# MLP weights fetched in 14 pieces spread over steps, in place of four transfers back to back

## Chip, cores, metric

The kernel runs on one core of a Trainium2 chip. The metric is the device time of one execution in microseconds (us); a run is an execution timed alone, and the profile is one execution taken by the hardware profiler. A run counts as slow when it is more than 1.5% above the fastest of the same kernel.

## The reference

A transformer block with modulation (cut; `mod` is six rows of `silu(c) @ w_mod`):

```
h = layernorm(x) * (1 + ca) + sa
x = x + ga * attention(h)      # 32 query heads, 8 kv heads, last 512 keys of the caches, head size 128; then @ wo
h = layernorm(x) * (1 + cb) + sb
x = x + gb * (relu(h @ w1) @ w2)   # w1 512 x 1792, w2 1792 x 512
```

There are 2048 rows of 512, all in bfloat16. A fast path and a general path are in the program; these inputs take the fast path, and only it is dealt with here.

## The kernel before

The rows go in 4 blocks of 512, each with 32 heads: 128 steps, one for each head and block. In a step PE computes scores, projects q for the head two steps on, does P·V of the previous head and adds up to four "background" matmuls. The background is mostly the output projection, in groups of eight heads (`HQ = 8`):

```python
for s in range(NU):                      # NU = 128 steps
    run_tasks(s, 100)                    # loads, layer norms, ... that are due at step s
    ...                                  # cut: enqueue an output projection that is ready
    s_mms(s, 0)
    if s + QA < NU:
        q_mms(s + QA)
    s_mms(s, 1)
    if s >= 1:
        pv_mms(s - 1)                    # P.V of head s-1, division on DVE, transpose by DMA
    pop_bg(4)                            # up to four output-projection matmuls
```

A head's output is divided on DVE, and the SP queue then transposes it by DMA. All that goes through SP is issued in program order:

```python
def pv_mms(u):
    ...                                  # cut: 16 matmuls into o_ps, reciprocal
    kb.op(DVE, ... o_sb[u % NOS] ...)    # NOS = 4
    dma(oT[u % NOT][:, :, :], o_sb[u % NOS]..., f"oT{u % NOT}",
        reads=[R_o[u % NOS]], writes=[R_oT[u % NOT]], transpose=True)
    if (u + 1) % HQ == 0:
        wo_ready.append((u + 2, b, h // HQ))   # group of eight: usable two steps later
```

The MLP weights land in the tile that held the modulation weights (`wmw`). They are loaded at steps 60 and 64, long before the MLP, in four transfers of 896 KB:

```python
def load_w1():
    for i in range(2):
        f0, f1 = i * FC // 2, (i + 1) * FC // 2            # FC = 14
        dma(w1_sb[:, :, f0 * P:f1 * P], w1v[:, :, f0 * P:f1 * P], f"w1{i}", writes=R_w1[f0:f1] + R_wm)

def load_w2():
    for i in range(2):
        f0, f1 = i * FC // 2, (i + 1) * FC // 2
        dma(w2_sb[:, f0:f1, :], w2v[:, f0:f1, :], f"w2{i}", writes=R_w2[f0:f1] + R_wm)

add(60, load_w1)
add(64, load_w2)
```

`writes=... + R_wm` is there so that a load waits for the last reader of the modulation weights. It has a second effect: each load is now the latest writer of `R_wm`, and the next load must wait until it has landed. That wait is on SP, ahead of everything that SP issues later.

## Time and profile before

| | before |
|---|---|
| time, median of 3 runs | 570.52 us (569.95 to 571.03) |
| span of the profiled run | 568.2 us |
| PE busy | 553.0 us, 97% |
| PE's one named wait between 14 and 560 us | 2.1 us, for the DMA oT<-o |
| weight loads | 4 x 896 KB, 5.2 us to landing |

A line of the timeline gives start, length, engine, source line, operation, output<-inputs and count; in square brackets stands how long the engine was idle before it and what ended that. PE is matmul, DVE the vector engine, SPq the queue of SyncE. "To landing" is the time from the start of a DMA's issue until its data is there; the length of an SPq row is the issue alone. Where a row covers several instructions its length runs from the first to the last.

### The profile page before, as it was taken

The page shows a single profiled execution, that of the slowest core. Times are in us where ns is not written, and L with a number is a line of the kernel's source. Part 1 is how long each engine was busy: PE and PEld are TensorE (multiplying, and loading weights), DVE is VectorE, ACT ScalarE, POOL GpSimd, SP SyncE. Part 2 cuts the span into 40 slices and gives each one's busy share as a digit, 9 for nine tenths or more (in the row PEclk, how much of TensorE's full clock was granted, in tenths as well). Part 3 has the DMA queues.
Part 4 walks back from the last instruction along what each step waited for, and adds up shares of the span by engine and source line. Part 5 has one row for each costly group of instructions (what it writes and reads, how often), then busy time and mean ns, then how long its engine had stood idle before and what let it go on. Part 6 is the DMA issues. An engine that isn't in the chain of part 4 may idle for free.

```text
span 568.2 us, 9662 instructions
## 1 busy us (share of the span) xinstructions
PE 553.0 (97%) x4094; PEld 318.7 (56%) x4169; DVE 242.9 (43%) x532; ACT 347.3 (61%) x445; POOL 38.7 (7%) x41
## 2 busy tenths in 40 slices
PE   6999999999999999989999999999999999999997
PEld 5565555666655555546666555555555654444443
DVE  4344465533334655323336553333354438322133
ACT  2876666666666666656666666666666654432500
POOL 1000000002300000023000000330000000000000
PEclk8999999999999999999999999999999999999999
DMA  8795768331231145742321432121114220210001
GB/s 227 202 192 119 179 131 171 81 74 38 39 76 38 38 81 124 167 108 42 75 39 37 75 75 39 38 38 38 38 37 67 47 39 1 38 38 22 22 28 47
DMA packets 111620, 42.67 MB, mean 75 GB/s; under 512 B 94032, under 2 KB 111184, under 8 KB 111568
## 3 DMA queue, kind: packets, MB, share of 16 engines
q1 hardware_dynamic: 110752, 41.70, 34.4%
q8 instruction: 34, 0.56, 0.4%
q10 hardware_dynamic: 816, 0.26, 0.2%
q14 instruction: 18, 0.15, 0.1%
HBM read 18.35 MB, written 2.10 MB: 36 GB/s over the span
## 4 chain that ended last, share of the span: by engine, by line
PE 96%; DMA 2%; DVE 1%; issue 1%; ACTq 0%
PE psS L1350 28%; PE psO L1350 26%; PE psQ L1350 23%; PE psW L1350 19%; DMA oT<-o 1%; DMA x<-in_A_x_dram 1%; DVE st L1360 0%; PE psS L1353 0%; DVE hT L1397 0%; DVE PT L1631 0%; DVE PT L1632 0%; DVE mv L1361 0%; DVE o L1475 0%; ACTq L1296 0%; DVE xn L1371 0%
## 5 line engine op out<-in xcount | busy, mean ns | idle before, releaser
L1464 ACT ACTIVATE PT<-psS 128x1024 bf16<-128x1024 f32 x256 | 262.8, 1028 | 131.7 <-PE psS L1350 131.7
L1350 PE MATMUL psS<-qT,kT 128*128 128x512 bf16 x509 | 151.2, 379 | 0.2
L1350 PEld LDWEIGHTS psO<-v,PT 128*128 128x128 bf16 x2048 | 126.6, 98 | 30.2
L1350 PE MATMUL psO<-v,PT 128*128 128x129 bf16 x2048 | 137.0, 220 | 0.0
L1350 PE MATMUL psQ<-hT,wq 128*128 128x512 bf16 x507 | 130.8, 381 | 1.1 <-DVE hT L1397 1.1
L1474 DVE RECIPROCAL rinv<-psO 128x4 f32<-128x4 f32 x128 | 23.3, 182 | 234.5 <-PE psO L1350 234.5
L1350 PE MATMUL psW<-wo,oT 128*128 128x512 bf16 x451 | 118.1, 379 | 5.3 <-DMA oT<-o 2.1
L1475 DVE TENSOR_TENSOR o<-psO,rinv 128x512 bf16<-128x512 f32 x128 | 88.5, 691 | 4.7 <-DVE rinv L1474 0.3
L1350 PEld LDWEIGHTS psQ<-hT,wq 128*128 128x128 bf16 x508 | 49.7, 98 | 61.1 <-issue 1.0
L1350 PEld LDWEIGHTS psS<-qT,kT 128*128 128x128 bf16 x512 | 49.7, 98 | 59.5 <-ACT PT L1464 0.7
L1456 ACT ACTIVATE qT<-psQ 128x512 bf16<-128x512 f32 x127 | 75.4, 593 | 1.2 <-PE psQ L1350 1.2
L1350 PEld LDWEIGHTS psW<-wo,oT 128*128 128x128 bf16 x512 | 44.9, 98 | 35.4 <-DMA oT<-o 2.6
L1620 ACT ACTIVATE wq<-psS 128x512 bf16<-128x512 f32 x56 | 33.4, 597 | 49.2 <-PE psS L1350 49.2
L1497 DVE TENSOR_TENSOR acc<-psW,acc 128x512 f32<-128x512 f32 x48 | 33.1, 690 | 9.0 <-PE psW L1350 9.0
L1350 PE MATMUL psO<-wmw,wq 128*128 128x512 bf16 x136 | 31.0, 379 | 0.3
L1366 POOL TENSOR_TENSOR rstd<-rstd,cst 128x4 f32<-128x4 f32 (+2 forms) x9 | 8.6, 961 | 273.5 <-DVE rstd L1365 273.4
L1500 POOL TENSOR_TENSOR acc<-acc,gaf 128x512 f32<-128x512 f32 x12 | 15.2, 1268 | 171.0 <-DVE acc L1497 171.0
L1350 PE MATMUL psS<-h2T,wmw 128*128 128x512 bf16 x110 | 25.2, 379 | 0.1
L1350 PE MATMUL psS<-hT,wmw 128*128 128x512 bf16 x110 | 24.4, 379 | 0.1
L1631 DVE TENSOR_TENSOR PT<-psO,gbf 128x512 f32<-128x512 f32 x10 | 6.9, 691 | 40.2 <-PE psO L1350 40.2
L1360 DVE BATCH_NORM_STATS2 st<-x 128x6 f32<-128x512 bf16 x32 | 21.7, 680 | 4.6 <-DMA x<-in_A_x_dram 4.6
L1350 PEld LDWEIGHTS psO<-wmw,wq 128*128 128x128 bf16 x140 | 13.7, 98 | 16.5
(60 smaller groups left out, 168.8 us busy)
## 6 DMA issues: line engine op xcount, KB each, us to landing
wo<-in_A_wo_dram SPq DMA_DIRECT2D x4, 1024.0 KB, 5.9
wq<-in_A_wq_dram SPq DMA_DIRECT2D x7, 512.0 KB, 5.8
wmw<-in_B_w_dram SPq DMA_DIRECT2D x4, 896.0 KB, 5.2
wmw<-in_w_mod_dram SPq DMA_DIRECT2D x6, 512.0 KB, 5.2
oT<-o SPq DMA_TRANSPOSE x128, 2.4
out_dram<-PT SPq DMA_DIRECT2D x16, 128.0 KB, 1.7
x<-in_A_x_dram SPq DMA_DIRECT2D x3, 512.0 KB, 4.2
v<-in_A_v_cache_dram SPq DMA_DIRECT2D x8, 128.0 KB, 4.6
```

The lines of the kernel that those rows point to most:

```text
L1350: kb.op(PE, lambda e: e.matmul(out_ap, lhsT, rhs, start=start, stop=stop), reads=reads, group_writes=[R_b[k] for k in bk], signal=signal)
L1360: kb.op(DVE, lambda e: e.bn_stats(st[:, t, :], x_sb[:, t, :]), reads=[R_x[t]], writes=[R_st[t]])
L1366: kb.op(POOL, lambda e: e.tensor_tensor(rstd[:, sl], rstd[:, sl], cst[:, 0:1].to_broadcast([P, hi - lo]), op=ALU.pow), reads=R_rstd[sl] + ...
L1456: kb.op(ACT, lambda e: e.activation(qT[u % NQT][:, :], bank[bk], ACTF.Copy), reads=[R_b[bk]], writes=[R_qT[u % NQT]])
L1464: kb.op(ACT, lambda e: e.activation(PT[u % NPT][:, pr * 2:pr * 2 + 2, :], s_ps[pr][:, :, :], ACTF.Exp, scale=scale), reads=[R_b[pr * 2], R ...
L1474: kb.op(DVE, lambda e: e.reciprocal(rinv[:, u, :], o_ps[:, :, P]), reads=[R_b[5], R_b[6]], writes=[R_rinv])
L1475: kb.op(DVE, lambda e: e.tensor_tensor(o_sb[u % NOS][:, :, :], o_ps[:, :, 0:P], rinv[:, u, :].unsqueeze(2).to_broadcast([P, TPB, P]), op=A ...
L1497: kb.op(DVE, lambda e: e.tensor_tensor(acc[:, tl, :], bank[WBK], acc[:, tl, :], op=ALU.add), reads=[R_b[WBK], R_acc[tl]], writes=[R_acc[tl]])
L1500: kb.op(eng, lambda e: e.tensor_tensor(acc[:, tl, :], acc[:, tl, :], gaf[:, :], op=ALU.mult), reads=[R_acc[tl], R_ga], writes=[R_acc[tl]])
L1620: kb.op(ACT, lambda e: e.activation(h1T[b % 2][:, fc, :], bank[bk], ACTF.Relu), reads=[R_b[bk]], writes=[R_h1[b % 2][fc]], pre=all_events( ...
L1631: kb.op(DVE, lambda e: e.tensor_tensor(yt[i], bank[bk], gbf[:, :], op=ALU.mult), reads=[R_b[bk], R_gb], writes=[R_yt[i]], pre=pt_done if c ...
```

## The change

The intent: no large block of weight traffic in front of the transposes. It has three parts: smaller pieces (14 x 256 KB), no wait of one piece for another (`pre=wm_done`, a list of the old readers and writers of `R_wm` to wait for, in place of writing `R_wm`), and other steps (57-60, 65-68, 73-76, 81, 82).

```diff
-    def load_w1():
-        for i in range(2):
-            f0, f1 = i * FC // 2, (i + 1) * FC // 2
-            dma(w1_sb[:, :, f0 * P:f1 * P], w1v[:, :, f0 * P:f1 * P], f"w1{i}", writes=R_w1[f0:f1] + R_wm)
-
-    def load_w2():
-        ...                                   # likewise
+    wm_done = []
+
+    def load_mlp(i):
+        if not wm_done:
+            wm_done.extend(all_events(R_wm))
+        f0 = i % (FC // 2) * 2
+        if i < FC // 2:
+            kb.op(SP, lambda e: e.dma_start(w1_sb[:, :, f0 * P:(f0 + 2) * P], w1v[:, :, f0 * P:(f0 + 2) * P]), writes=R_w1[f0:f0 + 2], pre=wm_done, dma_sem=dsem(f"w1{f0}"))
+        else:
+            ...                               # likewise for w2
-    add(60, load_w1)
-    add(64, load_w2)
+    for i, s in enumerate([s for s in range(57, NU) if s % HQ in (1, 2, 3, 4)][:FC]):
+        add(s, lambda i=i: load_mlp(i))
```

More of the change, by code (lines that the diff above doesn't have):

```diff
@@ L1337, in load_wo @@
         dma(wo_sb[:, j * HQ:(j + 1) * HQ, :], wov[:, j * HQ:(j + 1) * HQ, :], f"wo{j}", writes=[R_wo[j]])
-    def load_w1():
-        for i in range(2):
-            f0, f1 = i * FC // 2, (i + 1) * FC // 2
-            dma(w1_sb[:, :, f0 * P:f1 * P], w1v[:, :, f0 * P:f1 * P], f"w1{i}", writes=R_w1[f0:f1] + R_wm)
-    def load_w2():
-        for i in range(2):
-            f0, f1 = i * FC // 2, (i + 1) * FC // 2
-            dma(w2_sb[:, f0:f1, :], w2v[:, f0:f1, :], f"w2{i}", writes=R_w2[f0:f1] + R_wm)
+    wm_done = []
[6 more added lines that the diff above has]
+        else:
+            kb.op(SP, lambda e: e.dma_start(w2_sb[:, f0:f0 + 2, :], w2v[:, f0:f0 + 2, :]), writes=R_w2[f0:f0 + 2], pre=wm_done, dma_sem=dsem(f"w2{f0}"))
     def mm(out_ap, lhsT, rhs, start, stop, reads, bk, signal):
```

## The prediction

> **What bounds the kernel now.** I read the busy table and slices, then PE's idle time by stretch, then the one stretch that stood out, from PE, the chain and the issuing queue. The page first:
>
> ```profile
> PE 553.0 (97%) x4094; PEld 318.7 (56%) x4169; DVE 242.9 (43%) x532; ACT 347.3 (61%) x445; POOL 38.7 (7%) x41
> PE   6999999999999999989999999999999999999997
> DMA  8795768331231145742321432121114220210001
> ```
>
> PE is the bound: 97%, ACT next at 61%, and PE's digits are 9 but for the first, the last and one in the middle (slice 18, some 241 to 256 us). PE is idle 568.2 - 553.0 = 15.2 us. Where that lies, from the table by stretch (the second column is the length, the third PE's busy time; DMA share and GB/s stand last):
>
> ```profile
> 0.00:14.20 14.20, 8.68 (x99) 7.89 (x101) 7.06 (x22) 3.14 (x5) 2.53 (x10) 0.83 0.89 227
> 241.00:250.00 9.00, 6.81 (x55) 3.95 (x55) 2.13 (x6) 4.86 (x6) 2.09 (x2) 1.00 0.56 146
> 250.00:350.00 100.00, 99.27 (x782) 59.20 (x795) 45.53 (x105) 69.11 (x86) 9.63 (x9) 1.00 0.30 54
> 550.00:568.20 18.20, 14.49 (x67) 6.38 (x66) 7.77 (x12) 0.00 (x0) 0.00 (x0) 1.00 0.13 44
> ```
>
> The start holds 14.20 - 8.68 = 5.5 us of idle, the end 18.20 - 14.49 = 3.7, the 9 us around 245 hold 2.2. The other 3.8 us are spread thinly (0.73 in the 100 us from 250 on), as short "issue" gaps and matmuls missing from the records. So 2.2 us is the one thing in the middle that a load can have caused. PE in order of time there:
>
> ```profile
> 242.78 1.07 PE L1350 MATMUL psO<-v,PT 128*128 128x129 bf16 x16
> 243.69 0.81 PE L1350 MATMUL psW<-wo,oT 128*128 128x512 bf16 x3
> 246.63 0.39 PE L1350 MATMUL psW<-wo,oT 128*128 128x512 bf16 x1 [2.14 <-DMA oT<-o]
> 246.86 0.59 PE L1350 MATMUL psS<-qT,kT 128*128 128x512 bf16 x2
> ```
>
> PE stops for 2.14 us before one output-projection matmul because a transposed head oT has not landed. The list of PE's waits has this entry just once ("PE psW L1350 <- DMA oT<-o: 2.1, 1, 2.1"), and between 14 and 560 us no other. Why it was late, from the chain and from the issuing queue:
>
> ```profile
> 239.45 0.92 PE psO L1350 x16
> 240.39 0.19 DVE rinv L1474
> 240.61 0.51 DVE o L1475
> 241.11 5.47 DMA oT<-o
> 246.63 0.39 PE psW L1350
> ```
>
> ```profile
> 221.58 5.51 SPq L1296 DMA_DIRECT2D wmw<-in_B_w_dram  x2
> 227.13 8.39 SPq L1295 DMA_TRANSPOSE oT<-o  x4
> 235.57 5.50 SPq L1296 DMA_DIRECT2D wmw<-in_B_w_dram  x2
> 241.11 4.90 SPq L1295 DMA_TRANSPOSE oT<-o  x3
> ```
>
> The transpose took 5.47 us from issue to landing; the median over all 128 is 2.4. It was issued right behind the second half of w2. The queue's own waits hold "SPq L1296 <- DMA wmw<-in_B_w_dram: 9.1, 2, 4.5": twice the second half of a weight waited some 4.5 us for the first half to land, since each load lists all of R_wm among its writes. That put the second half of w2 at about 240.5 us, just ahead of this transpose.
>
> **What the Trainium skill says.** "DMA: Bandwidth & Descriptors", section "Queues, rings and completion order": one sequencer's DMAs use one ring per engine, and "On each SDMA engine descriptors are consumed in ring order". The trace agrees: with 896 KB ahead, oT lands in 5.47 us, and in 241.0 to 244.5 as well as in the stall the DMA engines are well loaded (185 and 291 GB/s). The opposite order matters more below: at 42.9 and at 70.1 us an oT was issued and a 512 KB wq load followed it at once (44.12, 71.22); these landed in 2.5 and 2.4 us, undisturbed. Same page, "Anatomy of one DMA": waits are served on the issuing sequencer before dispatch, so a waiting DMA holds all behind it; the 5.5 us rows above agree. Its fit of 2.0 us plus bytes over 436 GB/s (for the other descriptor path) would give about 4.1 us for 896 KB; the trace has 5.2, so I use the trace. Same page, "Rules for kernel authors", advises large transfers for bandwidth; the change goes against that, but no bandwidth is scarce here (75 GB/s mean).
>
> **The change part by part.** A step is one head: scores, a projection, P·V of the head before, and up to four background matmuls; it takes 3.50 us (psO starts at 211.47, 214.97, 218.47). Step 64 does P·V of head 63 (psO at 239.45). Every eight heads an output projection starts at step 8k+1 with heads 0 to 3 of the group and takes 4 to 7 in step 8k+2, so the last head's oT, issued at step 8k, is needed at the end of 8k+2.
>
> Removed: the four 896 KB loads at steps 60 and 64, and their serial waits (9.1 us on the queue, not on PE). At step 64 the oT of head 63 now finds an empty ring. It is still issued at 241.11, as DVE finishes o then, and lands at 241.1 + 2.4 = 243.5 us. The stalled matmul is the fourth of its step: 243.69 + 0.81 = 244.5 us. That is 1.0 us of slack in place of 2.1 us of stall. Gain: 2.14 us, all on the path, since PE paces everything after: no later PE wait is named before 560 us.
>
> Added: 14 loads of 256 KB at steps 57-60, 65-68, 73-76, 81, 82. PE, ACT and DVE have the same instructions in the same order (I compared the two programs; only line numbers move there). SP has 10 more issues at about 0.5 us, 5 us over some 90 us of a queue that works about 1.2 us per 3.5 us step: hidden. Size of one piece: 512 KB of x at 279.83 landed in 4.1 us and 896 KB in 5.1, so 1.0 us per 384 KB and 2.8 us fixed; my estimate for 256 KB is 3.4 us to land and 0.7 us on the engines. An oT behind a piece then lands in some 3.1 to 3.5 us instead of 2.4 (behind that x load one took 3.3). It is not needed for at least a step: at 8k+1 to 8k+4 the oT behind the piece is of heads 0 to 3 of the next group, needed at step 8k+9 or later. The o buffers (four) give four steps, 14 us. The one urgent oT, of step 8k, has the piece behind it, which the two wq cases show costs 0.1 us or less. Each piece has its own semaphore and its waits were met long before (the modulation weights are last read at 36 us). The rows of a w1 piece are 512 B instead of 1792 B: seven pieces make 3584 rows where two made 1024. The last piece goes out in step 82, at about 239.45 + 18 x 3.5 = 302 us less the stall, 150 us before the first MLP matmul (459 us).
>
> Sum: -2.14 for the stall, +0.0 to 0.3 for anything the pieces delay; my central figure is -2.1. 570.52 - 2.1 = 568.4 us; span 568.2 - 2.1 = 566.1 us.
>
> **The rivals.** (1) The stall moves: with pieces at steps 65, 73 and 81, directly behind each urgent oT, one lands late if the engines share bandwidth rather than keep ring order. A piece is 0.7 us of engine time against 1.0 us of slack, so even full sharing costs about nothing; twice that at all three would cost 3 x 0.4 = 1.2 us, leaving 569.6. The wq cases speak against it. (2) The first piece stands right behind a layer-norm transpose (xnT issued at 211.37, landing in 4.4 us), for which DVE waits 2.43 us before hT at 215.75; that holds up the emptying of psO. DVE finished o at 217.31 there and the next P·V starts at 218.47, so 1.1 us of delay is free; only more reaches PE. Ring order says no delay; if xnT lost 2 us, PE would lose about 0.9: 569.3. (3) The loads were hidden anyway and nothing moves, 570.5: most of the load time is indeed hidden (the 896 KB pair at step 60 stalled nobody), but the 2.14 us is recorded on PE with the DMA as its releaser, so I hold this for noise only. (4) A larger gain: lower DMA contention elsewhere speeds PE up. PE is at 99% in the neighbouring 100 us, its clock is granted in full; at most some tenths.
>
> **Range and chances.** The runs of before spread from 569.95 to 571.03, so about half a microsecond either way; rivals 1 and 2 stretch the upper side by one. Range 567.4 to 569.7. Two per cent are 11.4 us: more than all the idle time of PE outside the first slice, so faster by over 2% has a chance of 0.005; slower needs several new stalls of a kind that nothing here shows, 0.01; same 0.985.
>
> **What would show it.** Right: PE's wait for oT is gone from its list; the stretch 241 to 250 has some 8.9 us of PE busy; slice 18 reads 9; the queue no longer waits for a weight load; the oT of head 63 lands in about 2.4 us, an oT behind a piece in about 3.3, a piece in about 3.4; MLP's first matmul moves from 459.3 to about 457.2. Wrong: a new PE wait for oT near 244, 272 or 300 us (rival 1), or for psO or hT near 216 to 222 (rival 2), or a landing of pieces well above 4 us, which would mean that 512 B rows are dear.

## The result, and the profile after

The changed kernel takes 568.12 us (median of 4 runs, 567.87 to 568.66) beside 570.59 us for the kernel before (4 runs, 569.95 to 571.03). The ratio is 0.9959, with a 95% interval of 0.9942 to 0.9976: 0.4% faster, clear of noise, well within 2%. A ratio here is the mean time of one kernel's fast runs over that of the other's of the same rounds, so it isn't quite the ratio of the medians. On a second chip it was 0.9954 (0.9939 to 0.997).

The busy table, the PE slices and the DMA slices of the kernel after:

```profile
PE 557.6 (98%) x4169; PEld 318.8 (56%) x4169; DVE 242.8 (43%) x532; ACT 347.5 (61%) x445; POOL 38.7 (7%) x41
PE   6999999999999999999999999999999999999997
DMA  9785768342232147242522532121224210200001
```

The 8 in slice 18 has become a 9. The table by stretch, with the columns that the prediction explains:

```profile
241.00:250.00 9.00, 9.00 (x71) 5.22 (x70) 2.62 (x6) 6.26 (x8) 2.43 (x2) 1.00 0.47 117
250.00:350.00 100.00, 100.00 (x805) 59.57 (x803) 46.18 (x107) 69.04 (x86) 9.30 (x8) 1.00 0.36 72
```

PE now has no idle time in the 9 us around 245. The second row explains the thin idle time in the prediction: the trace of before holds 4094 of 4169 matmul records, this one all of them, and here the same kind of stretch is 100% busy. That "spread" idle time was missing records, not gaps. PE in order of time:

```profile
242.70 1.07 PE L1351 MATMUL psO<-v,PT 128*128 128x129 bf16 x16
243.61 1.03 PE L1351 MATMUL psW<-wo,oT 128*128 128x512 bf16 x4
244.47 0.59 PE L1351 MATMUL psS<-qT,kT 128*128 128x512 bf16 x2
```

All four projection matmuls run without a break. From the psW row to the next psS row it is 244.47 - 243.61 = 0.86 us, and before it was 246.86 - 243.69 = 3.17 us. So the stall had cost 2.31 us, a little more than its recorded 2.14: the recorded wait starts at the end of the third matmul, and matmuls in a row overlap in the record (three take 0.81 us, four 1.03), so that the fourth would have started before that end. That agrees with the times: 0.41% of 570.6 is 2.3 us.

The issuing queue after, and the DMA issues by kind:

```profile
237.75 1.19 SPq L1295 DMA_TRANSPOSE oT<-o  x1
238.99 0.58 SPq L1346 DMA_DIRECT2D wmw<-in_B_w_dram  x1
241.25 1.19 SPq L1295 DMA_TRANSPOSE oT<-o  x1
```

```profile
wmw<-in_B_w_dram SPq DMA_DIRECT2D x14, 256.0 KB, 3.1
oT<-o SPq DMA_TRANSPOSE x128, 2.4
```

The transpose at 237.75 us is head 63, the last of its group of eight, directly followed by the first piece of step 65. Here the trace contradicts the prediction, which had this transpose issued at 241.11 us in both kernels "as DVE finishes o then". DVE around it in the kernel before:

```profile
237.11 0.69 DVE L1475 TENSOR_TENSOR o<-psO,rinv 128x512 bf16<-128x512 f32 x1
237.76 0.69 DVE L1497 TENSOR_TENSOR acc<-psW,acc 128x512 f32<-128x512 f32 x1
240.39 0.18 DVE L1474 RECIPROCAL rinv<-psO 128x4 f32<-128x4 f32 x1 [1.94 <-PE psO L1350]
240.61 0.69 DVE L1475 TENSOR_TENSOR o<-psO,rinv 128x512 bf16<-128x512 f32 x1
```

Counting the transposes in the queue's order shows that the one at 241.11 belongs to head 63, and head 63 was divided at 237.11 and finished at 237.80. The division at 240.61 is head 64's. It ends at 241.30, after the transpose was issued, so it cannot have released it. The chain of waits had named the nearest DVE event in time. The real reason is one row up in the queue: SP sat in the wait for the first half of w2.

So two delays stood one on the other, and head 63 had more slack than I said. "Hold" is the time for which SP kept the transpose back, "ring" the delay by what had been issued on SP ahead of it and had not landed:

- Hold: SP issued head 63 at 241.11 instead of 237.80, 3.31 us late.
- Ring: it landed 5.47 us after its issue instead of 2.4, 3.07 us more, as the second half of w2 was ahead of it.
- Slack: it would have landed at 237.80 + 2.4 = 240.2 us and was needed at 243.69 + 0.81 = 244.5 us, which is 4.3 us.
- Sum: 3.31 + 3.07 - 4.3 = 2.1 us of stall. PE recorded 2.14.

I call this theory A. If it is right, neither delay reaches PE by itself, and any of several smaller edits would do what the 14 pieces do. The rivals: (B) large transfers close together are the cost, so it takes pieces, or (E) spreading; (C) the hold alone is the cause; (D) the hold matters and the bytes ahead don't.

### The profile page after: what moved, and what is told of

Its sections match the earlier page's. It is cut to its first block, busy times and chain, and to the rows that moved or that the text cites. A ratio compares the mean times of both kernels' runs of the same rounds, so it can differ in the third digit from the quotient of the medians.

```text
span 566.1 us, 9753 instructions
## 1 busy us (share of the span) xinstructions
PE 557.6 (98%) x4169; PEld 318.8 (56%) x4169; DVE 242.8 (43%) x532; ACT 347.5 (61%) x445; POOL 38.7 (7%) x41
## 4 chain that ended last, share of the span: by engine, by line
PE 98%; DVE 1%; DMA 1%; issue 0%; ACTq 0%
PE psS L1351 28%; PE psO L1351 26%; PE psQ L1351 23%; PE psW L1351 20%; DMA x<-in_A_x_dram 1%; DVE st L1361 0%; PE psS L1354 0%; DVE PT L1632 0%; DVE PT L1633 0%; DVE mv L1362 0%; DVE hT L1398 0%; ACTq L1296 0%; DVE xn L1372 0%; DVE rstd L1366 0%; DVE tmp L1410 0%
## 5 line engine op out<-in xcount | busy, mean ns | idle before, releaser
L1351 PE MATMUL psW<-wo,oT 128*128 128x512 bf16 x512 | 130.6, 379 | 0.0
```

The source lines that it names most:

```text
L1351: kb.op(PE, lambda e: e.matmul(out_ap, lhsT, rhs, start=start, stop=stop), reads=reads, group_writes=[R_b[k] for k in bk], signal=signal)
```

## The experiments

Four kernels ran on one chip with five rounds each (e1 to e4), then e5, e6 and e7 with the changed kernel again on another, then e8. All passed the check of the outputs (see e7 for what that check does not see).

**e1: the four large transfers at their old steps, without the waits for each other.**

```diff
-            dma(w2_sb[:, f0:f1, :], ..., f"w2{i}", writes=R_w2[f0:f1] + R_wm)
+            kb.op(SP, ..., writes=R_w2[f0:f1], pre=wm_done, dma_sem=dsem(f"w2{i}"))     # w1 likewise
```

> The four 896 KB loads at their old steps, but each waits only for the modulation weights to have been read, so no half waits for the other half. Theory A (two delays add: the queue was held 3.3 us by the wait for the first half of w2, and the ring then held 896 KB ahead; sum 6.4 us against 4.3 us of slack of the transposed head 63): no hold now, head 63 is issued at about 237.8 us, lands at 243 to 244 behind 1792 KB, needed at 244.5, so no PE wait for oT and 568.2 us (567.6 to 568.9). Rival B (large transfers bunched together are the cost, so splitting and spreading is needed): PE still waits about 2 us, 570.5.

Measured: 568.34 us, ratio 0.9952 (0.9939 to 0.9965). PE has no wait for oT. The queue of e1 (its start took 0.9 us longer in the profiled run, so all its times are later by that):

```profile
236.43 1.19 SPq L1350 DMA_DIRECT2D wmw<-in_B_w_dram  x2
238.69 1.20 SPq L1295 DMA_TRANSPOSE oT<-o  x1
```

and PE in e1, without a break:

```profile
244.55 1.03 PE L1353 MATMUL psW<-wo,oT 128*128 128x512 bf16 x4
```

Head 63 was ready at 238.66 and issued at 238.69, with no hold; it landed 6.2 us later, 3.8 more than alone. That is below 4.3, by half a microsecond. Two transfers of 896 KB close together cost no time here: rivals B and E fall.

**e2: one digit.** The kernel before, with w2 loaded a step later and all waits kept.

```diff
-    add(64, load_w2)
+    add(65, load_w2)
```

> The kernel before with w2 loaded at step 65 in place of 64, one digit, serial waits and large transfers kept. Theory A: the transposed head 63 is issued ahead of w2 at 237.8 us and lands in 2.4 us; the transposes held behind w2 are not needed for seven steps: no PE wait for oT, 568.2 us (567.6 to 568.9). Rival B (bunched large transfers): still about 570.5. Rival C (any queue hold of 3 us or more reaches PE): still about 570.5.

Measured: 567.88 us, ratio 0.9946 (0.9934 to 0.9958). The queue of e2:

```profile
237.78 1.19 SPq L1295 DMA_TRANSPOSE oT<-o  x1
239.02 5.45 SPq L1296 DMA_DIRECT2D wmw<-in_B_w_dram  x2
244.51 11.95 SPq L1295 DMA_TRANSPOSE oT<-o  x5
```

Head 63 goes out ahead of w2 and lands in 2.5 us. The queue is held as long as ever, but now it is head 64 that waits, and that is not needed for seven steps. This one digit gives all that the change gives.

**e3: the hold without the bytes.** Only the first half of w2 at step 64, then a wait for it, then head 63.

```diff
-    add(64, load_w2)
+    add(64, lambda: (load_w2(0), SP.ops.append((lambda e: e.nop(), [("w20", 16)], []))))
+    add(65, lambda: load_w2(1))            # cut: load_w2 now takes the half that it loads
```

> At step 64 only the first half of w2, then the queue waits for its landing, then head 63 is transposed; the second half goes out at step 65. The hold stays, the 896 KB ahead in the ring are gone. Theory A: head 63 is issued at about 240.6 us, lands at about 243.0, 1.5 us before it is needed: no PE wait for oT, 568.2 us (567.6 to 568.9). Rival C (the hold of the queue alone is the cause): PE still waits, 569.5 to 570.5.

Measured: 568.25 us, ratio 0.9953 (0.994 to 0.9967), and no wait of PE for oT. The queue of e3:

```profile
235.52 0.58 SPq L1296 DMA_DIRECT2D wmw<-in_B_w_dram  x1
240.70 1.19 SPq L1295 DMA_TRANSPOSE oT<-o  x1
```

and PE in e3:

```profile
243.64 1.03 PE L1350 MATMUL psW<-wo,oT 128*128 128x512 bf16 x4
```

Head 63 was issued at 240.70, about as late as before, and landed in 2.5 us. The hold alone is 2.95 us and does not reach PE: rival C falls.

**e4: the bytes without the hold.** As e1, but all four loads at step 64 (`add(64, load_w1)`).

> All four loads, 3584 KB, at step 64 back to back with no wait between them: no hold, four times the bytes in the ring ahead of head 63. Theory A: issued at about 238 us, lands after the loads, at 235.6 + 2.8 + 9.3 = 247.7 us or a little later, needed at 244.5: PE waits 3 to 4 us for oT, 571.2 to 572.6 us. Rival D (only the hold matters; small transposes pass loads in the ring): no PE wait, 568.2.

Measured: 574.93 us, ratio 1.0067 (1.0054 to 1.008), slower than the kernel before. PE in e4:

```profile
243.67 0.81 PE L1353 MATMUL psW<-wo,oT 128*128 128x512 bf16 x3
249.26 0.61 PE L1353 MATMUL psW<-wo,oT 128*128 128x512 bf16 x1 [4.78 <-DMA oT<-o]
249.66 1.06 PE L1353 MATMUL psS<-qT,kT 128*128 128x512 bf16 x2
250.52 1.91 PE L1353 MATMUL psQ<-hT,wq 128*128 128x512 bf16 x4
```

Rival D falls: bytes ahead in the ring do stall PE (there is a small hold here too; e8, which has none, shows it alone). My range was missed on two counts. Four issues took SP until 239.13, so there was a small hold of 1.34 us too, and with a landing of 10.09 us the sum is 1.34 + 7.69 - 4.3 = 4.7 us (recorded: 4.78). And after the stall the matmuls took nearly twice as long for a step. The table by stretch has the granted clock in the third column from the right:

```profile
244.50:249.20 4.70, 0.00 (x0) 0.00 (x0) 0.28 (x1) 0.00 (x0) 0.00 (x0) 0.91 1.19 305
249.20:255.50 6.30, 6.24 (x28) 3.40 (x29) 1.10 (x3) 2.64 (x3) 2.42 (x2) 0.53 0.06 11
255.50:258.00 2.50, 2.50 (x19) 1.32 (x18) 0.46 (x1) 1.52 (x3) 0.00 (x0) 1.00 0.26 52
```

For 6.3 us the clock was 0.53. From the row at 243.67 to the projection matmuls of the next step, at 254.81, it took 11.14 us in place of 3.50. So 7.6 us were lost in the profiled run, the slowest of e4's six: some 4.9 in the stall, counted as for the kernel before, and 2.7 in the slower matmuls. The Trainium skill, "TensorE: Matmul & The Clock Gate", Part 1, says that PE falls back to half its clock after an idle window of some 3.4 us; this run agrees, and the stall of 2.14 us in the kernel before, after which the clock stayed at 1.00, agrees too.

**e5: small pieces with the old waits, bunched.** Seven pieces at step 60 and seven at 64, each writing `R_wm` again.

> 14 pieces of 256 KB as in the changed kernel, but seven at step 60 and seven at step 64, and each waiting for the piece before it to land (the old list of writes). Same bytes, small pieces, much longer holds of the queue. Theory A: the queue is held some 6 x 3.1 = 19 us from 221.5 on; head 59 is transposed at about 240.7, so the ring of four o buffers stops DVE and then PE for 5 to 6 us at head 63; then the seven w2 pieces hold head 63 to about 267 us, against a need at about 250: another 19 us. With the matmul clock lost after long idleness some 590 to 602 us. Rival B (it is large transfers that cost; small pieces don't): no PE wait for oT, 568 to 570 us.

Measured: 590.02 us, ratio 1.0333 (1.0313 to 1.0353), 21.8 us more than the changed kernel beside it. PE in e5:

```profile
242.70 1.92 PE L1351 MATMUL psO<-v,PT 128*128 128x129 bf16 x16 [3.19 <-DVE o L1476]
248.58 0.81 PE L1351 MATMUL psW<-wo,oT 128*128 128x512 bf16 x3
263.71 0.61 PE L1351 MATMUL psW<-wo,oT 128*128 128x512 bf16 x1 [14.31 <-DMA oT<-o]
```

and its queue:

```profile
221.64 17.07 SPq L1346 DMA_DIRECT2D wmw<-in_B_w_dram  x7
238.75 5.12 SPq L1295 DMA_TRANSPOSE oT<-o  x4
243.91 16.71 SPq L1348 DMA_DIRECT2D wmw<-in_B_w_dram  x7
260.67 28.61 SPq L1295 DMA_TRANSPOSE oT<-o  x9
```

The same bytes, in pieces of the same size as in the changed kernel, hold the queue twice for 17 us. The first hold reaches PE by way of the four o buffers: DVE waits 4.8 us for the transpose that frees one, and PE waits for DVE. The second delays head 63 to 260.67. From one piece's issue to the next it took 2.7 to 2.8 us, not 3.1 as I had set, and so the time stands at the lower edge of what theory A expected. The two waits of PE make 17.5 of the 21.8 us. Most of the rest is the clock: it was 0.50 from 242.70 to 244.80 us, where the 16 matmuls of the first row took 1.92 us in place of 1.07, and 0.53 from 263.70 to 270.00. So an idle time of 3.19 us already cost clock. Cutting a transfer into pieces that wait for each other multiplies the hold; B is wrong in sign here.

**e6: the pieces and waits of the changed kernel, bunched at steps 60 and 64.**

> The 14 pieces of the changed kernel with its waits, but bunched, seven at step 60 and seven at step 64. Theory A: seven issues take 4.1 us, so head 63 is issued at about 239.7 (1.9 us late), and lands behind 1792 KB at 243 to 244, needed at 244.5: no PE wait for oT, 568.2 us (567.6 to 569.3). Rival E (the spreading over steps is what gains): 570 or more.

Measured: 568.55 us, ratio 0.996 (0.9945 to 0.9976). PE in e6:

```profile
243.65 0.81 PE L1351 MATMUL psW<-wo,oT 128*128 128x512 bf16 x3
244.67 0.39 PE L1351 MATMUL psW<-wo,oT 128*128 128x512 bf16 x1 [0.21 <-DMA oT<-o]
244.90 0.59 PE L1351 MATMUL psS<-qT,kT 128*128 128x512 bf16 x2
```

The seven issues hold head 63 until 239.23, 1.47 us late, and it lands in 5.40, 3.0 over: 4.47 less 4.3 makes 0.2 us of stall, and 0.21 was recorded, where I had expected none. Counted from the psW row to the psS row, as above, it is 244.90 - 243.65 = 1.25 us against 0.86: spreading the pieces over steps is worth some 0.4 us in the trace, not the 2.3. In the medians it is 0.3 us (568.26 for the changed kernel beside it), which is within the noise.

**after_again: the changed kernel beside e5, e6 and e7.**

> The changed kernel again, beside the others on this chip: 568.2 us, ratio 0.995 to 0.9965 to the kernel before; theories A and B agree.

Measured: 568.26 us, ratio 0.9954 (0.9939 to 0.997), as expected.

**e7: a side question.** In reading the trace I found that both kernels overwrite `xnT`. The first layer norm of block 2 is transposed into it (issued at 204.15 us in the kernel before), the second layer norm of block 0 overwrites it (issued at 211.37, landing 4.4 us later), and only then, at 215.75, DVE makes block 2's hT from it; blocks 3 and 1 stand the same way. The program asks for this order, so no race is reported; the recorder orders accesses but cannot know which value was meant. e7 moves the later layer norm on four steps:

```diff
-        add_ln(b, 2, H * (b + 1) + 19)
+        add_ln(b, 2, H * (b + 1) + (23 if b < NB - 2 else 19))
```

> The changed kernel with the second layer norm of blocks 0 and 1 four steps later, so that its transpose no longer writes xnT before the first layer norm of blocks 2 and 3 has read it (in both kernels the program order has it overwritten first). Both theories: the loads are not concerned, 568.2 us (567.4 to 569.2), result correct as before; DVE's long waits for xnT ahead of hT should get shorter.

Measured: 568.10 us, ratio 0.9955 (0.9935 to 0.9976), and correct. The order costs nothing to mend. That block 2's values were wrong is read from the order of instructions; the check of the outputs passes either way, so it does not see it, and no run here compared the values themselves. DVE's waits for xnT ahead of hT fell from 9.1 to 4.3 us in total, off PE's path.

**e8: the same stall from another mixture.** As e1, but with the second half of w1 at step 64 too, so three loads of 896 KB there and no hold.

> Three 896 KB loads at step 64 with no wait between them (the first half of w1 stays at step 60): bytes between e1 (1792 KB, no stall) and e4 (3584 KB, 4.78 us). The landing of head 63 moved from about 244.0 to 249.2 us between those two, 2.6 us for each 896 KB, so here about 246.6, against a need at 244.5. Theory A: PE waits 1.8 to 2.4 us for oT, no loss of clock as in the kernel before, 570.2 to 571.2 us: the same loss as before by another mixture, no hold and more bytes. If the loss of time were from the hold alone, 568.2. If any stall of this length also cost clock, 572 or more.

Measured: 571.15 us, ratio 1.0009 (0.9996 to 1.0021), equal to the kernel before. PE in e8:

```profile
244.08 0.81 PE L1354 MATMUL psW<-wo,oT 128*128 128x512 bf16 x3
247.13 0.39 PE L1354 MATMUL psW<-wo,oT 128*128 128x512 bf16 x1 [2.24 <-DMA oT<-o]
247.36 0.59 PE L1354 MATMUL psS<-qT,kT 128*128 128x512 bf16 x2
```

The rows after the stall are as short as ever (psS 0.59, in e4 1.06), so 2.24 us idle did not cost the clock.

All of this in one table. "Late" is the issue of head 63 less the end of its division on DVE; "over" is its time to landing less 2.4 us; the slack is 4.3 us.

| kernel | ready | issued | late | landing | over | late + over - 4.3 | PE's recorded wait | time us |
|---|---|---|---|---|---|---|---|---|
| before | 237.80 | 241.11 | 3.31 | 5.47 | 3.07 | 2.1 | 2.14 | 570.6 |
| after | 237.73 | 237.75 | 0.02 | 2.5 | 0.1 | below 0 | none | 568.1 |
| e1, no hold, 1792 KB | 238.66 | 238.69 | 0.03 | 6.2 | 3.8 | below 0 | none | 568.3 |
| e2, a step later | 237.75 | 237.78 | 0.03 | 2.5 | 0.1 | below 0 | none | 567.9 |
| e3, hold alone | 237.75 | 240.70 | 2.95 | 2.5 | 0.1 | below 0 | none | 568.3 |
| e6, bunched pieces | 237.76 | 239.23 | 1.47 | 5.40 | 3.00 | 0.2 | 0.21 | 568.6 |
| e8, 2688 KB | 238.20 | 238.22 | 0.02 | 8.86 | 6.46 | 2.2 | 2.24 | 571.2 |
| e4, 3584 KB | 237.79 | 239.13 | 1.34 | 10.09 | 7.69 | 4.7 | 4.78 | 574.9 |

Eight kernels, and the sum gives each recorded wait within 0.1 us. In part that is bookkeeping, since late and over together only say when head 63 landed; it shows that this landing alone sets the wait. That two delays make it up is shown by e3 and e1, which take away one of them each. Between e1, e8 and e4, each further 896 KB ahead moved the landing by about 2.6 us (e1 and e8 set to the same start).

## Why the prediction was right, and where it was not

- The time (568.4 predicted, 568.1 measured), the span (566.1 and 566.1) and the gain (2.1 predicted, 2.3 measured) were right, and for the reason given as far as it goes: one stall of PE behind a late oT, caused by the w2 load, goes away, and PE paces all that follows. How the load made oT late was only half seen (next point). The first MLP matmul moved from 459.3 to 456.9 us (457.2 predicted). The stall costs 2.31 us on PE's timeline and not the recorded 2.14.
- The step that failed is "It is still issued at 241.11, as DVE finishes o then". I took 239.45 for head 63's P·V; it is head 64's, and head 63's is at 235.95. The issue moved to 237.75. With it fell "1.0 us of slack in place of 2.1 us of stall": the slack is 4.3 us. The total was not touched, as a stall that is gone is gone with either slack. I had seen the 9.1 us of queue waits and used them only to place the second half of w2; their other half, the 3.3 us by which they held the transpose itself, is missing from the sum.
- Rival 1, a stall behind a piece at steps 65, 73 or 81: did not happen; no PE wait for oT is left. With 4.3 us of slack it was much further off than I thought.
- Rival 2, the first piece slowing the layer-norm transpose: that transpose landed in 4.4 us in both, as ring order had it.
- Rivals 3 (nothing moves) and 4 (a larger gain): neither; the gain of 2.3 us is what the stall cost.
- "An oT behind a piece lands in some 3.1 to 3.5 us": ten of the 14 took 2.4 to 2.5, being issued about 2 us after the piece, when the piece has nearly landed. A piece lands in 3.1 us at the median, not 3.4. The other four took 2.7, 2.9, 3.7 (behind the x load as well) and 4.5; this last one follows a layer-norm transpose too, and behind that alone it had taken 4.6 in the kernel before.
- Rows of 512 B in the w1 pieces cost nothing that shows. The page count of packets went from 111620 to 114340.

## What to carry to other kernels

When a consumer waits for a small DMA, work out its slack first (ready, alone to landing, needed), then add what its queue held it back for and what lay ahead of it in the ring; here neither of the two delays, at its size, reached PE alone, and both together did. A resource that is listed as written only in order to wait for its old readers also makes the writers wait for each other, and an in-order queue turns that into a hold on everything behind. Before cutting a transfer into pieces, try moving it by one step: one digit gave the whole gain, and pieces that wait for each other cost 22 us.

## What the Trainium skill lacked or had wrong

- "DMA: Bandwidth & Descriptors", Anatomy of one DMA: its fit of 2.0 us plus bytes over 436 GB/s is for transfers issued from GpSimd; none is given for those from SP. On SP, 896 KB landed in 5.1 to 5.2 us in the kernel before (an estimate by the fit: 4.1) and a piece of 256 KB in 3.1 at the median (an estimate by the fit: 2.6).
- The same page, Queues, rings and completion order, has what ring order means but no figure for a small transfer behind a large one. Here a 128 KB transpose that lands in 2.4 us alone took 5.5 behind an 896 KB load issued 0.4 us earlier, and each further 896 KB, from 1792 KB on, added about 2.6 us. A load issued right behind a transpose did not slow it (2.4 to 2.5 us for heads 63 to 65 in the changed kernel).
- The same page gives a bandwidth for DMA transposes but no time for a small one, and does not say that the issue itself can grow with what is queued ahead: 1.19 us on SP normally, 4.91 us for the transpose behind 3584 KB in e4.
- "TensorE: Matmul & The Clock Gate", Part 1: its window of some 3.4 us agrees in the main. 2.24 us of idle left the clock at full speed; 4.78 us cost 6.3 us at 0.53 of it. But 3.19 us of idle in e5 already brought it to 0.50.
- No page warns that the releaser named in a chain of waits can be the nearest event in time rather than the real one: here it named a division that ended at 241.30 us as what released a transpose issued at 241.11.
